# Casts of P at the head of ScalarE's step, homes behind low parts, and a two-pass hash with row groups added by VectorE, in an LSH attention kernel with an FFN

## The chip, the cores and the metric

One Trainium2 chip, of which the kernel uses one core. The metric is the device time of the kernel in microseconds (us), the median of several runs. Before the change it is 975.12 us (three runs, 974.37 to 977.23). The engines are named as in the profile: PE (matmul) and PEld (its weight loads), DVE (VectorE), ACT (ScalarE), POOL (GpSimd), SP (the sync engine, whose queue issues nearly all transfers).

## The reference

The kernel computes LSH attention and a gated FFN on its result. There are 4 batches of 8 heads, 768 positions and 64 channels.

```python
q_bits = (np.einsum('bhsd,dk->bhsk', q, proj) > 0)      # 6 bits
k_bits = (np.einsum('bhsd,dk->bhsk', k, proj) > 0)
mask = q_bucket[:, :, :, None] == k_bucket[:, :, None, :]
scores = np.where(mask, scale * np.matmul(q, k.transpose(0, 1, 3, 2)), -1e9)
attn = np.exp(scores - np.max(scores, axis=-1, keepdims=True))
attn = attn / (np.sum(attn, axis=-1, keepdims=True) + 1e-09)
x = np.matmul(attn, v)          # then to [3072 tokens, 512]
h = x @ w_in                    # 512 x 2048
g = h * np.clip(h + 3.0, 0.0, 6.0) / 6.0
return g @ w_out                # 2048 x 512
```

A query and a key belong to one bucket when their six sign bits agree.

## The kernel before, in words

**Numbers in two parts.** Every float32 operand of a matmul is split into a high part, rounded to the matmul's own type `F32R` by a cast, and a low part, the difference. Products are made of high x high, high x low and low x high. A "cast" below is the making of a high part, on ACT; a "low part" is the subtraction behind it, on DVE or POOL.

**The hash.** A head's queries and keys lie in two tiles of 2 x 768 columns, `kk` and `qq`. Their halves are `k1`, `k2`, `q1`, `q2` (L287). `q1` holds the high parts of the scaled queries in rows 0 to 63 and of the keys in rows 64 to 127, `k2` the low and high parts of the keys, `q2` the high and low parts of the queries. `hash_qk` (L325) makes the projections of one half of the columns by three passes of 384 columns: low weights on `q1`, high weights on `k2`, high weights on `q2` (L334 to L336). `bits` (L340) turns their signs into twelve rows for the queries and twelve for the keys, which are appended to the operands of the scores, so that a bucket that differs makes a score huge. On DVE this is one compare-and-multiply a half (L352), whose rows for the keys go to `k1` by a transfer (L359).

**Tiles of attention.** A head has six tiles of 128 queries; `g` counts all 192 of them. A tile takes scores on PE (L387, L389), the minimum and a cap on DVE (`lowest`, L396), the exponential with its sums on ACT (`exponential`, L408). Then P has to be transposed for the value products. In the first half of the kernel PE does that (L418). From tile 102 (`GT`) on it goes through memory: `flip` (L426) transposes 32x32 blocks on DVE (L429) and writes the tile to a scratch tensor `fd` (L431, 384 KB), and `move` (L434) brings it home by four transfers of 96 KB each, which put the blocks in place (L444). There are two homes, `spare` and `px`, for even and odd tiles. `split_p` (L451) casts a home in two halves on ACT (L475); the low part of half 1 is made on POOL (L477) and that of half 0 on DVE (L479). `values_whole` (L505) multiplies two tiles at a time with V (L513).

**The FFN beside it.** The batches 1 to 3 have nine chunks of 256 tokens, and a chunk has 16 slices of the hidden width. A slice is GEMM1 (L661, 12 matmuls of 256 columns), the gate (a relu on ACT, L683, and a product on DVE, L684), the gate's cast and low part (L689 on ACT, L690 on DVE), and GEMM2 (L699 to L704, six matmuls of 512 columns), which runs a slice later. The generator `ffn` (L927) gives such a slice in parts, named A to D: A the gate's cast and low part, B the next GEMM1, C the GEMM2 of the slice before and the relu, D the work on the next chunk's input.

**The order.** The order on PE, DVE, ACT and POOL is the order of the program text; on SP a scheduler places the transfers, within the bounds that `issue_after` sets. Each engine and SP's queue work in order. From tile 102 on, `beside_ffn(k)` (L1115) writes one step per tile (90 of them): value products (odd k), `lowest(k+2)`, part A, `exponential(k+2)`, `flip(k+2)`, cast of half 1 of tile k-1, part B, copies of finished values, in one step of six the hash, part C with the cast of half 0 of tile k-1 and its low part behind the relu (the list `amid`, L1174, called from `gate` at L685), then `lead(k+3)` (L1038: scores, and by turns the split, load and scaling of later heads), `move(k+1)` and part D. The list `moves` holds transfers that are issued one a step (L1183).

Of the kernel before, what the change touches and what calls it, by code (L numbers as in the profile page):

```python
# [10 lines left out]
F32 = mybir.dt.float32  # L11
# [32 lines left out]
def lsh_attention_moe(  # L44
# [74 lines left out]
    pjl = cp.tile([P, ZM], F32R, name="pjl")  # L119
    pjh = cp.tile([P, ZM + ZK - D], F32R, name="pjh")  # L120
    nc.vector.memset(pjl[:].bitcast(F32), 0.0)
    nc.vector.memset(pjh[:].bitcast(F32), 0.0)
    pjk, pjq = pjh[:, :ZM], pjh[:, ZK - D :]


    nc.vector.memset(thr[:], 0.0)
    nc.vector.memset(val[:], 0.0)
    for r, one, big in ((D, 0, -BIG), (ZK, 1, 1.0)):
# [4 lines left out]
        nc.vector.memset(val[r : r + NB], big * (1, -1)[one])  # L133
    nc.vector.memset(three[:], 3.0)

    raw0 = sp.tile([P, S], F32, name="raw0", tag="raw", bufs=1)[:]
# [142 lines left out]
    subs = []  # L279
    moves = []  # L280

# [43 lines left out]
    def hash_qk(i: int):  # L325
        k1, k2, q1, q2 = state[i]
        if paced:
            z = zs[i] = [bank([P, HW], f"z{i}_{j}") for j in range(2)]
        else:
            both = pair(f"z{i}")  # L330
            z = zs[i] = [both[:, j, :HW] for j in range(2)]
        for j in range(2):
            c = slice(j * HW, (j + 1) * HW)
            nc.tensor.matmul(z[j][:ZM], lhsT=pjl[:], rhs=q1[:, c], start=True, stop=False)  # L334
            nc.tensor.matmul(z[j][:ZM], lhsT=pjk, rhs=k2[:, c], start=False, stop=False)
            nc.tensor.matmul(z[j][:ZM], lhsT=pjq, rhs=q2[:, c], start=False, stop=True)  # L336
        if not paced:
            zs[i] = both

    def bits(i: int):  # L340
# [3 lines left out]
        if isinstance(z, list):  # L344
            whole = [(slice(j * HW, (j + 1) * HW), z[j][D:ZM], False) for j in range(2)]
        elif i == 0:
# [76 lines left out]

    written, moved, homes = {}, {}, []

    def flip(g: int):  # L426
# [3 lines left out]
        d = dp.tile([P, S], F32, name=f"fd{g}", tag="fd", bufs=4)  # L430
        dma(out=d[:], in_=x)  # L431
        written[g] = d, last

    def move(g: int):  # L434
# [6 lines left out]
        with tc.issue_after(after.ins):  # L441
            for x in range(4):
# [86 lines left out]
    def output(un: int):  # L529
# [18 lines left out]
        if u or last_head:  # L548
# [6 lines left out]
            if not last_head:  # L555
                ts = (u,) if single or u else (0, 1)
                (fresh if single and u == 2 else adds).append((i, ts if u != 1 or single else (0, 1), to, y[r2] if single else outs[i][r2]))
        vdone = 2 * un + 2
# [168 lines left out]
    xr0, x0 = {}, {}  # L727
    side, opening, amid = [], [], []

# [197 lines left out]
    def ffn():  # L927
# [49 lines left out]
        for c, (b, t) in enumerate(chunks):  # L977
# [21 lines left out]
            for fc in range(NFC):  # L999
# [6 lines left out]
                parted = paced  # L1006
                split_g = gate(n, fc, hp, copy, nc.vector, lambda: amid and amid.pop()())
                if not parted:
# [29 lines left out]
    def lead(j: int):  # L1038
# [11 lines left out]
        if t == (3 if paced else 2):  # L1050

            if n + 1 < NJ and n != H + 1:
                get_qk(n + 1)
                if paced:
                    get_k_rows(n + 1)
        if t == (5 if paced else 3) and n < NJ:
# [42 lines left out]
    with tc.manual_schedule(engines={ET.PE, ET.DVE, ET.Activation, ET.Pool}):  # L1099
# [15 lines left out]
        def beside_ffn(k: int):  # L1115
# [9 lines left out]
            for _ in range(2):  # L1125
# [45 lines left out]
            if hashed:  # L1171
                hash_qk((k + LA) // KT + 1)
            if split:
                amid.append(lambda: (split_p(k - LT, 0, False), split_lows()))  # L1174
            go("C")
            while amid:
                amid.pop()()
            split_lows()
            if hashed:
                bits((k + LA) // KT + 1)  # L1180
            if k + LA < NS:
# [13 lines left out]
        for k in range(NS + LT + 2):  # L1195
# [11 lines left out]
            if k == HK:  # L1207
                late["x"] = sp.tile([P, S], F32, name="late", tag="raw", bufs=1)
            for c in range(2):
                transp(k, c)  # L1210
# [117 lines left out]
```

## Time and profile before

| | |
|---|---|
| median of three runs | 975.12 us |
| the profiled execution | 973.11 us, span 971.3 us, granted PE clock 0.998 |
| attention alone, first FFN, attention to tile 101 | about 0 to 395 us |
| attention beside the FFN, tiles 102 to 191 | about 395 to 805 us |
| FFN alone | about 805 to 971 us |
| PE busy, 395 to 805 us | 403.18 us |
| DVE, ACT, POOL busy there | 324.57, 272.67, 211.39 us |
| DMA engines busy there | 82%, 240 GB/s |

A row of a group reads: line, engine, operation, out<-in by the program's names, shapes, count, then the busy time in us, the mean of one in ns, and the idle time of the engine before it with what ended it. PE's busy time is modelled and its matmuls overlap, so the start times of neighbouring rows tell what a matmul costs. SP's rows are issues of transfers; how long a transfer flies is seen only where something waits for it. A wait for several things is put down to the one that came last.

### The profile page before, as it was taken

The numbers are of one execution on the slowest core, as the hardware profiler recorded it, in microseconds if no ns is written. First come the engines' busy times: TensorE is split into PE (matmuls) and PEld (weight loads), VectorE is DVE, ScalarE is ACT, GpSimd is POOL, SyncE is SP. The second block draws the span as 40 slices with busy tenths as digits, with TensorE's granted clock in tenths as the row PEclk, the third lists the DMA queues.
The fourth block names the chain that finished last, engine by engine and source line by source line (L and its number), as shares of the span: only waits on it lengthen the run. The fifth ranks groups of instructions, "written<-read, shape, count | busy, mean of one in ns | idle before, by whom it ended". The sixth has DMA issues, their size and how long they took to land.

```text
span 971.3 us, 19460 instructions
## 1 busy us (share of the span) xinstructions
PE 948.0 (98%) x6306; PEld 873.6 (90%) x6306; DVE 723.5 (74%) x1470; ACT 625.0 (64%) x1421; POOL 473.6 (49%) x582
## 2 busy tenths in 40 slices
PE   8999999999999999899999999999999999999997
PEld 7999888999989999799899899989899899889896
DVE  7999988888569999877878878878777874342422
ACT  6898875655478988667766666666666664333332
POOL 6777744665537776455555545555545432000000
PEclk9999999999999999999999999999999999999999
DMA  3567579100035554787898788788887772101000
GB/s 117 140 156 188 131 224 377 58 1 1 6 119 119 115 142 112 192 252 233 238 267 234 231 256 241 230 267 236 243 258 233 211 227 71 44 1 44 1 22 22
DMA packets 113613, 152.06 MB, mean 157 GB/s; under 512 B 13876, under 2 KB 82612, under 8 KB 113512
## 3 DMA queue, kind: packets, MB, share of 16 engines
q1 hardware_dynamic: 108472, 144.79, 48.8%
q0 software_dynamic: 5040, 6.03, 5.3%
q8 instruction: 50, 0.82, 0.4%
q14 instruction: 51, 0.42, 0.2%
HBM read 77.34 MB, written 54.00 MB: 135 GB/s over the span
## 4 chain that ended last, share of the span: by engine, by line
PE 79%; DVE 8%; DMA 4%; ACT 4%; issue 3%; POOL 1%; SPq 1%; ACTq 0%; DVEq 0%; POOLq 0%
PE h L661 25%; PE acc L500 6%; PE po L704 6%; PE po L699 6%; PE po L700 6%; PE acc L513 6%; PE pt L418 5%; PE s L389 5%; PE s L387 5%; DMA spare<-fd 2%; DVE p L396 2%; DVE pl L479 2%; ACT ph L475 1%; SPq L78 1%; DVE qq L352 1%
## 5 line engine op out<-in xcount | busy, mean ns | idle before, releaser
L408 ACT ACTIVATE p<-p,m 128x768 f32<-128x768 f32 x192 | 180.2, 939 | 113.4 <-DVE p L396 105.2
L396 DVE TENSOR_SCALAR_CACHE_REDUCE p<-s 128x768 f32<-128x768 f32 x192 | 182.7, 952 | 24.9 <-PE pt L418 12.4
L684 DVE SCALAR_TENSOR_TENSOR h<-g,h 128x256 f32<-128x256 f32 x192 | 81.1, 423 | 102.0 <-ACT g L683 99.0
L683 ACT ACTIVATE g<-h,three 128x256 f32<-128x256 f32 x192 | 91.2, 475 | 94.9 <-PE h L661 94.0
L661 PE MATMUL h<-xh,w 128*128 128x256 f32 x1024 | 146.8, 282 | 0.0
L661 PEld LDWEIGHTS h<-xh,w 128*128 128x128 f32 x1024 | 134.9, 188 | 4.2 <-ACT xh L650 0.6
L429 DVE STREAM_TRANSPOSE p<-p 128x768 f32<-128x768 f32 x90 | 88.1, 979 | 65.2 <-ACT p L408 65.1
L477 POOL TENSOR_TENSOR pl<-spare,ph 128x384 fp32r<-128x384 f32 x45 | 45.8, 1018 | 127.3 <-ACT ph L475 71.4
L479 DVE TENSOR_TENSOR pl<-pt,ph 128x384 fp32r<-128x384 f32 x196 | 100.0, 550 | 4.0 <-ACT ph L475 3.5
L387 PE MATMUL s<-kk,qq 76*128 76x384 f32 x384 | 100.5, 343 | 2.0 <-ACT kk L357 1.5
L389 PE MATMUL s<-kk,qq 128*128 128x384 f32 x384 | 100.4, 343 | 0.0
L700 PE MATMUL po<-w,gb 128*128 128x512 f32 x250 | 98.4, 393 | 0.0
L699 PE MATMUL po<-w,gb 128*128 128x512 f32 x250 | 98.3, 393 | 0.0
L475 ACT CAST ph<-pt 128x384 fp32r<-128x384 f32 x196 | 86.1, 474 | 14.3 <-PE pt L418 13.0
L216 POOL TENSOR_TENSOR w<-wr,w 128x128 fp32r<-128x128 f32 x128 | 71.9, 593 | 45.2 <-ACT w L210 41.9
L418 PE MATMUL pt<-ident,p 128*128 128x128 f32 x612 | 86.2, 275 | 1.9 <-DVE pl L479 1.1
L689 ACT CAST gb<-h 128x256 fp32r<-128x256 f32 x141 | 52.4, 372 | 54.5 <-DVE h L684 26.8
L661 PE MATMUL h<-xl,w 128*128 128x256 f32 x512 | 81.2, 280 | 0.0
L418 PEld LDWEIGHTS pt<-ident,p 128*128 128x128 f32 x612 | 72.5, 141 | 8.9 <-PE pt L418 1.5
L704 PE MATMUL po<-w,gb 128*128 128x512 f32 x250 | 78.6, 395 | 1.5 <-DVE gb L690 1.5
L318 POOL TENSOR_TENSOR kk<-raw,qq 64x192 fp32r<-64x192 f32 (+1 forms) x73 | 65.4, 920 | 25.1 <-ACT qq L304 21.7
L387 PEld LDWEIGHTS s<-kk,qq 76*128 76x128 f32 x384 | 66.6, 190 | 11.7 <-ACT kk L357 2.0
(153 smaller groups left out, 2150.9 us busy)
## 6 DMA issues: line engine op xcount, KB each, us to landing
fd<-p SPq DMA_DIRECT2D x90, 384.0 KB
spare<-fd SPq DMA_DIRECT2D x180, 96.0 KB
px<-fd SPq DMA_DIRECT2D x180, 96.0 KB
kk<-qq SPq DMA_DIRECT2D x62, 192.0 KB
wr<-in_w_in SPq DMA_DIRECT2D x16, 512.0 KB
wr<-in_w_out SPq DMA_DIRECT2D x16, 512.0 KB
raw<-in_qkT SPq DMA_DIRECT2D x19, 384.0 KB
vr<-in_v SPq DMA_DIRECT2D x32, 192.0 KB
```

Of the source, the lines that this page charges most:

```text
L387: nc.tensor.matmul(s[:, c, :HW], lhsT=q1[:KM, us], rhs=half(k1[:KM], c), start=True, stop=False)
L389: nc.tensor.matmul(s[:, c, :HW], lhsT=q2[:, us], rhs=half(k2, c), start=False, stop=True)
L396: nc.vector.tensor_scalar(out=pr_[:], in0=s[:, :, :HW], scalar1=CAP, scalar2=None, op0=ALU.min, op1=ALU.min, accum_out=m[:],)
L408: nc.scalar.activation(pr_[:], pr_[:], AF.Exp, bias=m[:], scale=-1.0, accum_out=sms[b][:, t, h : h + 1])
L418: nc.tensor.transpose(pt[:, x], probs[g][0][:, c, x * P : (x + 1) * P], ident[:])
L475: nc.scalar.copy(hi, pt)
L479: lows.append(lambda: engine.tensor_sub(lo, pt, hi.bitcast(F32)))
L661: nc.tensor.matmul(hp, lhsT=wi[:, wp, wc], rhs=x[cc][xp], start=(k == 0 and cc == 0), stop=(k == 2 and cc == NCC - 1),)
L683: nc.scalar.activation(r[:], hp, AF.Relu, bias=three[:], scale=1.0)
L699: nc.tensor.matmul(po[u], lhsT=gh[:, us], rhs=wo[:, 0], start=(fc == 0), stop=False)
L700: nc.tensor.matmul(po[u], lhsT=gh[:, us], rhs=wo[:, 1], start=False, stop=False)
L704: nc.tensor.matmul(po[u], lhsT=gl[:, us], rhs=wo[:, 0], start=False, stop=(fc == NFC - 1))
```

## The change

There are three edits to the steps beside the FFN, and what they need.

1. **Casts first.** In `beside_ffn`, both casts of tile k-1 stand at the head of ACT's step, ahead of the gate's cast and of the exponential, and the low part of half 0 (DVE) right behind them, ahead of the gate's low part. In the step behind a hash the gate's cast and low part stand between the casts and the low part of P. The list `amid` is gone. In the first such step (k = 103) the casts stand at the end.
2. **Homes behind low parts.** `move(k+1)` follows the low parts of tile k-1 at once, instead of standing at the step's end. `flip(k+2)` comes later in the same step, and its transfer to `fd` is ordered behind the last of the four homes (`brought`). The transfer of the keys' bits and the load of the next keys' rows wait in a list `behind_home`, which is emptied at the step's end; the keys' rows are loaded a step later than before.
3. **The hash in two passes.** Beside the FFN, `short_weights` makes a weight tile `pjs` (in the room of `pjh`) on POOL, once, at step 100. One pass is made on `q2` and one on `k2`. Each weight has 120 columns: 24 for the products with low weights and 24, at row 96, for those with high weights. ACT copies the first group of rows from the result into rows 96 to 119 of the next head's raw tile, DVE adds the second group there, and one compare-and-multiply over all 768 columns makes the bits. Its limits and factors (`limits`) are set by eight memsets on POOL at the start.

Beside these, the accumulating transfer for the last third of a head (L557) goes into the list that is sent next, not into the one behind it.

```diff
 def get_k_rows(i):
-        moves.append(lambda: dma(out=raws[i][D:], in_=qkT[b, h, D:]))
+        behind_home.append(lambda: dma(out=raws[i][D:], in_=qkT[b, h, D:]))
...
+    def short_weights():
+        pjs = cp.tile([P, ZK + NR + NQ], F32R, name="pjs", tag="pjh")
+        nc.gpsimd.memset(pjs[:].bitcast(F32), 0.0)
+        short.extend([pjs[:, : ZK + NR], pjs[:, NQ:]])
+        c = ZK + NQ
+        pos = pjs[:, c + NB : c + NQ].bitcast(F32)
+        for x in range(2):
+            nc.gpsimd.tensor_scalar_mul(pjs[:, c + (1 - x) * NB : c + (2 - x) * NB], pr[:], (1.0, -1.0)[x])
+        nc.gpsimd.tensor_sub(pjs[:, NQ + NB : 2 * NQ], pr[:], pos)
+        nc.gpsimd.tensor_sub(pjs[:, NQ : NQ + NB], pos, pr[:])
...
 def hash_qk(i):
         if paced:
-            z = zs[i] = [bank([P, HW], f"z{i}_{j}") for j in range(2)]
+            zs[i] = []
+            for j in range(2):
+                c = slice(j * HW, (j + 1) * HW)
+                z = bank([P, HW], f"z{i}_{j}")
+                zs[i].append(z)
+                nc.tensor.matmul(z[: ZK + NR], lhsT=short[1], rhs=q2[:, c], start=True, stop=False)
+                nc.tensor.matmul(z[: ZK + NR], lhsT=short[0], rhs=k2[:, c], start=False, stop=True)
+            return
...
 def bits(i):
         if isinstance(z, list):
-            whole = [(slice(j * HW, (j + 1) * HW), z[j][D:ZM], False) for j in range(2)]
+            r = slice(ZK, ZK + NR)
+            both = raws[i + 1][r] if i + 1 < NJ else sp.tile([P, S], F32, name=f"raw{i + 1}", tag="raw", bufs=1)[r]
+            for j in range(2):
+                nc.scalar.copy(both[:, j * HW : (j + 1) * HW], z[j][:NR])
+            for j in range(2):
+                c = slice(j * HW, (j + 1) * HW)
+                nc.vector.tensor_add(both[:, c], z[j][r], both[:, c])
+            nc.vector.tensor_scalar(
+                out=q1[D : D + NR], in0=both, scalar1=ths[r], scalar2=vas[r], op0=ALU.is_gt, op1=ALU.mult,
+            )
+            behind_home.append(lambda: dma(out=k1[D : D + NQ].bitcast(F32), in_=q1[D + NQ : D + NR].bitcast(F32)))
+            return
...
 def flip(g):
-        dma(out=d[:], in_=x)
+        if brought:
+            with tc.issue_after(brought.pop().ins):
+                dma(out=d[:], in_=x)
+        else:
+            dma(out=d[:], in_=x)
...
 def move(g):
+        brought[:] = [last]
...
 def beside_ffn(k):
-            behind = (k - 1 + LA) % KT == 4
-            if GT <= k < NS - 2 and not behind:
+            split = GT <= k - LT < NS
+            if not split or k == GT + 1:
+                go("A")
+            if GT <= k < NS - 2:
                 lowest(k + 2)
-            go("A")
-            if GT <= k < NS - 2 and behind:
-                lowest(k + 2)
+            if split and k - LT > GT:
+                multiply()
+                for c in (1, 0):
+                    split_p(k - LT, c, False)
+                if (k - 1 + LA) % KT == 4:
+                    go("A")
+                split_lows()
+                if k + 1 < NS:
+                    move(k + 1)
+                go("A")
...
-            split = GT <= k - LT < NS
-            if split:
-                split_p(k - LT, 1, False)
             go("B")
...
-            if split:
-                amid.append(lambda: (split_p(k - LT, 0, False), split_lows()))
             go("C")
-            while amid:
-                amid.pop()()
-            split_lows()
...
-            if GT <= k + 1 < NS:
+            if GT <= k + 1 < NS and not (split and k - LT > GT):
                 move(k + 1)
+            while behind_home:
+                behind_home.pop(0)()
```

How this moves the instructions is seen at three places. The first is SP's queue around the tiles 133 to 135. `fd133` is tile 133's scratch tensor, `p133` the tile itself, `spare` and `px` are the homes, `raw`, `xs` and `vr` other traffic. Before:

```order
L78 DMA fd133_7383<-p133_7375 128x768
L78 DMA spare_5091<-fd132_7317 32x4x192 x4
L78 DMA raw24_7472<-in_qkT 64x768 x2
L78 DMA xs2_127<-y21_0_7334 64x512
L78 DMA fd134_7442<-p134_7434 128x768
L78 DMA px_5555<-fd133_7383 32x4x192 x4
L78 DMA fd135_7509<-p135_7501 128x768
```

And with the change:

```order
L78 DMA fd133_7415<-p133_7395 128x768
L78 DMA xs2_136<-y21_0_7360 64x512
L78 DMA px_5570<-fd133_7415 32x4x192 x4
L78 DMA fd134_7470<-p134_7454 128x768
L78 DMA vr23_7644<-in_v 128x384
L78 DMA spare_5100<-fd134_7470 32x4x192 x4
L78 DMA fd135_7540<-p135_7520 128x768
```

Before, the homes behind `fd134` read `fd133`, which was issued a step earlier. Now they read the `fd` that was issued last, and the next `fd` stands behind them.

The second place is ACT in the same steps: `ph65` holds the high parts of the tiles 130 and 131, `g` and `h` are the gate, `gb` its high part, `y` finished values. Before, from the cast of the gate on:

```order
L689 CAST gb1_1_13_7436<-h1_1_13_7389 128x256
L408 ACTIVATE p134_7434,sms2_5285<-p134_7434,m134_7433 128x768
L475 CAST ph65_1_7385<-px_5555 128x3x128
L547 COPY y21_0_7334<-acc64_7361 128x256
L683 ACTIVATE g1_1_14_7467<-h1_1_14_7446,three_68 128x256
L475 CAST ph65_0_7411<-px_5555 128x3x128
```

With the change:

```order
L517 CAST ph65_1_7398<-px_5570 128x3x128
L517 CAST ph65_0_7402<-px_5570 128x3x128
L731 CAST gb1_1_13_7465<-h1_1_13_7417 128x256
L445 ACTIVATE p134_7454,sms2_5294<-p134_7454,m134_7453 128x768
L589 COPY y21_0_7360<-acc64_7381 128x256
L725 ACTIVATE g1_1_14_7493<-h1_1_14_7472,three_68 128x256
```

Both casts of the home have moved from behind the exponential and from behind the relu to the head, and the gate's cast and the exponential stand behind them.

The third place is PE at the hash of head 23, between GEMM1 and GEMM2. Before:

```order
L334 MATMUL z23_0_7528<-qq_23_7286,pjl_74 108x384
L335 MATMUL z23_0_7528<-kk_23_7285,pjh_75 108x384
L336 MATMUL z23_0_7528<-qq_23_7286,pjh_75 108x384
L334 MATMUL z23_1_7529<-qq_23_7286,pjl_74 108x384
L335 MATMUL z23_1_7529<-kk_23_7285,pjh_75 108x384
L336 MATMUL z23_1_7529<-qq_23_7286,pjh_75 108x384
L699 MATMUL po1_1_6590<-w29_3343,gb1_1_14_7503 128x512
```

With the change:

```order
L354 MATMUL z23_0_7555<-qq_23_7310,pjs_5485 120x384
L355 MATMUL z23_0_7555<-kk_23_7309,pjs_5485 120x384
L354 MATMUL z23_1_7558<-qq_23_7310,pjs_5485 120x384
L355 MATMUL z23_1_7558<-kk_23_7309,pjs_5485 120x384
L741 MATMUL po1_1_6614<-w29_3352,gb1_1_14_7535 128x512
```

Two of six passes are gone, and GEMM2 follows the fourth.

More of the change, by code (lines that the diff above doesn't have):

```diff
@@ L119, in lsh_attention_moe @@
     pjl = cp.tile([P, ZM], F32R, name="pjl")
-    pjh = cp.tile([P, ZM + ZK - D], F32R, name="pjh")
+    pjh = cp.tile([P, ZM + ZK - D], F32R, name="pjh", tag="pjh")
     nc.vector.memset(pjl[:].bitcast(F32), 0.0)
@@ L123, in lsh_attention_moe @@
     pjk, pjq = pjh[:, :ZM], pjh[:, ZK - D :]
+    NQ = 2 * NB
+    NR = 2 * NQ
+    short = []
+    limits = cp.tile([P, 2], F32, name="limits")
+    ths, vas = limits[:, 0:1], limits[:, 1:2]
     nc.vector.memset(thr[:], 0.0)
@@ L327, in hash_qk @@
         if paced:
-            z = zs[i] = [bank([P, HW], f"z{i}_{j}") for j in range(2)]
-        else:
-            both = pair(f"z{i}")
-            z = zs[i] = [both[:, j, :HW] for j in range(2)]
+            zs[i] = []
[6 more added lines that the diff above has]
+            return
+        both = pair(f"z{i}")
+        z = zs[i] = [both[:, j, :HW] for j in range(2)]
         for j in range(2):
@@ L336, in hash_qk @@
             nc.tensor.matmul(z[j][:ZM], lhsT=pjq, rhs=q2[:, c], start=False, stop=True)
-        if not paced:
-            zs[i] = both
+        zs[i] = both
     def bits(i: int):
@@ L556, in output @@
                 ts = (u,) if single or u else (0, 1)
-                (fresh if single and u == 2 else adds).append((i, ts if u != 1 or single else (0, 1), to, y[r2] if single else outs[i][r2]))
+                (fresh if single and u == 2 and not paced else adds).append((i, ts if u != 1 or single else (0, 1), to, y[r2] if single else outs[i][r2]))
         vdone = 2 * un + 2
@@ L727, in lsh_attention_moe @@
     xr0, x0 = {}, {}
[L728 removed]
+    side, opening = [], []
     def beside():
@@ L1006, in ffn @@
                 parted = paced
-                split_g = gate(n, fc, hp, copy, nc.vector, lambda: amid and amid.pop()())
+                split_g = gate(n, fc, hp, copy, nc.vector)
                 if not parted:
```

20 lines of the change are left out of this document (15 added, 5 removed).

## Prediction

> **What bounds the kernel now.** I read the page first, then the stretch in which attention runs beside the FFN (395 to 805 us), because all of the change but two tiny set-up pieces lies there.
>
> ```profile
> span 971.3 us, 19460 instructions
> PE 948.0 (98%) x6306; PEld 873.6 (90%) x6306; DVE 723.5 (74%) x1470; ACT 625.0 (64%) x1421; POOL 473.6 (49%) x582
> ```
>
> ```profile
> 395.00:805.00 410.00, 403.18 (x2614) 371.45 (x2613) 324.57 (x620) 272.67 (x639) 211.39 (x273) 1.00 0.82 240
> ```
>
> The second fence is that stretch in the table of windows: its length, then PE, PEld, DVE, ACT and POOL busy, then the granted clock, the DMA engines' busy share and GB/s. PE is busy 403 of 410 us at full clock; VectorE 79%, ScalarE 67%; but the DMA engines are busy 82% too. So PE paces, and the transfers come next. The waits of PE and of its weight loads in this stretch say what is left to win:
>
> ```profile
> PE acc L513 <- ACT ph L475: 4.5, 9, 1.5
> PE po L704 <- DVE gb L690: 1.5, 2, 0.8
> PEld acc L513 <- ACT ph L475: 6.0, 12, 1.7
> ```
>
> (Total us, times, longest.) The value products wait for the casts of P, 6.0 us counted at the weight load; everything else is small. A step's length comes from the transfer that each step issues once, in the view of the tile `fd`, and the homes that bring it back, four to a step:
>
> ```profile
> L78 SPq DMA_DIRECT2D fd<-p x89: 320/382/1419, 400.4 to 800.8; - x89
> L78 SPq DMA_DIRECT2D spare<-fd x180: 302/442/887, 400.8 to 803.1; - x180
> ```
>
> 89 issues from 400.4 to 800.8 are 88 steps of 4.55 us. The queue that issues them waits as follows (its own waits in the stretch):
>
> ```profile
> SPq L78 <- DVE pl L479: 25.7, 55, 1.0
> SPq L78 <- DMA fd<-p: 3.2, 6, 0.8
> ```
>
> Today homes wait for the low part that frees their buffer (55 times), and almost never for the landing of `fd`, because each home's source was issued a step before it. This second row is the one that I expect to change.
>
> **The hash.** A hash in this stretch is six passes; here is one from the timeline (start, us), and behind it the groups of the stretch by line (count, busy, mean ns):
>
> ```profile
> 763.38 0.34 PE L334 MATMUL z<-qq,pjl 128*108 128x384 f32 x1
> 763.56 0.34 PE L335 MATMUL z<-kk,pjh 128*108 128x384 f32 x1
> 763.74 0.34 PE L336 MATMUL z<-qq,pjh 128*108 128x384 f32 x1
> ...
> 764.43 0.40 PE L699 MATMUL po<-w,gb 128*128 128x512 f32 x1
> ```
>
> ```profile
> L334 PE MATMUL z<-qq,pjl 128*108 128x384 f32 x28 | 9.5, 338 | 0.2 <-ACT y L547 0.2
> L352 DVE TENSOR_SCALAR qq<-z,thr,val 44x384 fp32r<-44x384 f32 x28 | 18.0, 686 | 0.5
> ```
>
> From 763.38 to 764.43 six passes take 1.05, so 0.175 each (the 338 ns of a row overlap). x28 is two halves of 14 heads; two passes less a head are 14 x 2 x 0.175 = 4.9 us of PE, all on its path. Added are two copies of 24x384 on ScalarE, two sums and one compare on VectorE:
>
> ```profile
> L475 ACT CAST ph<-px 128x384 fp32r<-128x384 f32 x88 | 44.2, 502 | 0.4 <-issue 0.2 <-DMA px<-fd 0.2
> L479 DVE TENSOR_TENSOR pl<-px,ph 128x384 fp32r<-128x384 f32 x44 | 28.5, 648 | 0.1
> L429 DVE STREAM_TRANSPOSE p<-p 128x768 f32<-128x768 f32 x90 | 88.1, 979 | 65.2 <-ACT p L408 65.1
> L408 ACT ACTIVATE p<-p,m 128x768 f32<-128x768 f32 x89 | 83.5, 939 | 101.9 <-DVE p L396 94.2 <-DMA spare<-fd 6.3 <-DMA fd<-p 1.4
> L408 ACT ACTIVATION_READ_ACCUMULATOR p<-p,m 128x1 f32 x89 | 16.5, 186 | 0.0
> L689 ACT CAST gb<-h 128x256 fp32r<-128x256 f32 x89 | 33.0, 371 | 28.3 <-PE po L704 24.0 <-DVE h L684 1.6
> ```
>
> By nearest shapes, ScalarE pays 2 x 0.5 = 1.0 and VectorE 2 x 0.65 + about 1.0 (768 wide, as the transpose) - 2 x 0.69 = 0.9 more per head, once in six steps (27 us) in which VectorE is idle 21% and ScalarE 33%, 5.6 and 9. I cost it at nothing; were the cover gone it would be at most 14 x 1.0 = 14 us, below nothing I see no way. The two passes need the shifted rows and the low parts of both operands at once, where the first of three needed only `q1`; the third needed them 0.35 us later anyway, so: nothing. The load of the next K rows now waits, on the sync queue and ahead of a home, until the compare has read its scratch rows; that lies inside the flight of `fd` (below) as long as the queue runs late, and would else hold a home by about 1 us a head, within the slack worked out below. The K rows themselves are loaded a step later, behind the homes, and are needed two steps on, 9 us for a transfer like v's (2.1 us, below): nothing. The short weights and eight memsets run on POOL, and the last accumulating transfer of a head is sent one turn earlier there; POOL is 49% busy: nothing.
>
> **The casts and the value products.** With both casts at the head of ScalarE's step and the low parts behind them, the products that need them a step later find them ready: up to 6.0 us back. What moves behind is the cast of the gate (L689), by 2 x 0.50 us, and the exponential. The gate's cast is needed behind a whole GEMM1, so at full pace this costs nothing. But ScalarE works in order: when a home is late, the cast waits, and behind it now stand the gate's cast (GEMM2 waits for it) and the exponential (the next `fd` waits for it). Before, only the relu stood behind the first cast.
>
> **The homes and fd.** Here I see the price. Today the queue runs fd(g+1), home(g): a home's source has a whole step to land. In the change it runs fd(g), home(g), fd(g+1): a home waits for the `fd` just issued, and the next `fd` stands behind those homes. One turn of this chain is the flight of `fd`, F, and the issue of four homes. No turn starts before the last has ended, so on average no step can be shorter than one turn. The four issues from the queue's timeline, and a flight there:
>
> ```profile
> 413.47 1.89 SPq L78 DMA_DIRECT2D px<-fd  x4
> ...
> 447.71 0.53 SPq L78 DMA_DIRECT2D fd<-p  x1
> 448.49 2.83 SPq L78 DMA_DIRECT2D px<-fd  x4
> 451.42 0.38 SPq L78 DMA_DIRECT2D fd<-p  x1
> 452.65 1.75 SPq L78 DMA_DIRECT2D spare<-fd  x4
> ```
>
> Four homes take 1.75 to 1.89 when nothing holds them; I take 1.89, with 0.05 before and behind them. The homes at 452.65 had waited for the `fd` of 447.71 (the longest wait, 0.8, of the six): F was there 452.65 - 447.71 = 4.9, an upper end, with other homes in flight beside it. The trace shows no flight of a lone `fd`, so it is bounded from smaller transfers in the chain that ended last (start, us from issue to landing), and the best rate of the DMA view:
>
> ```profile
> 516.88 1.78 DMA spare<-fd
> 527.59 2.12 DMA spare<-fd
> 546.67 2.08 DMA vr<-in_v
> 575.82 3.53 DMA spare<-fd
> GB/s 230 247 223 275 204 253 218 246 258 274 254 265 203 234 237 224 255 262 253 260 210 231 232 271 259 236 243 252 215 254 279 247 255 224 242 215 182 270 208 212
> ```
>
> A home (96 KB) lands in 1.78 to 3.53, v (192 KB) in 2.08. `fd` has 384 KB: 288 KB (294,912 B) more than a home at 279 GB/s are 1.06, so 2.84; from v, 192 KB more are 0.70, so 2.78. The least would be a home's 1.78, the most 4.9. I take 2.7, just under the two sums, since little else flies beside it now. In the Trainium skill, "DMA: Bandwidth & Descriptors", section "Anatomy of one DMA", a transfer costs about 2.0 us whatever its size plus bytes over 436 GB/s (a fit for the other, software path), mostly the receipt from the target memory. By that, estimated, F would be 2.9 and the sum below would end 18 us later, inside case (4). No run here shows a lone flight, but the 1.78 of a home is under that 2.0.
>
> One turn: 2.7 + 0.05 + 1.89 + 0.05 = 4.69, against 4.55 now and against PE's own pace with all gains, (88 x 4.55 - 4.9 - 6.0) / 88 = 4.43. Until the chain is felt, slack runs out first: a step's casts to the issue of its `fd` are 2 x 0.50 + 0.37 + 0.94 + 0.19 + 0.98 = 3.5 (casts of P and of the gate, exponential, its sum, transpose); then F, the fourth home's start 1.89 - 0.44 later and its landing in 2.1, as at 527.59: 9.8 in all. The casts that need it stand three steps on, 13.3 at 4.43: 3.5 are left.
>
> Sum on the profiled execution (973.1, 1.8 of it outside the span): 88 x (4.69 - 4.55) = +12.3, less 3.5 = +8.8, so 982. PE's 10.9 us are in this, since the chain's turn takes the place of PE's pace. The median of the runs was 975.1, 2.0 above the profiled one, so the median I name is 984.
>
> **The rivals.** (1) PE keeps the pace: F is at most 4.43 - 1.99 = 2.44. Then both gains come whole, 975.1 - 10.9 = 964. For it: PE's 98%, and the 1.78 of a small transfer. Against: both sums from rows put 384 KB over 2.7, at the best rate. 0.15. (2) The chain paces, but turns fast: F from 2.44 to 2.57, 964 to 972; the row of 55 waits for low parts speaks for it, since those waits go. 0.18. (3) No change: F around 2.6, where 88 x (4.59 - 4.55) meets the slack of 3.5. A measurement of this kernel can tell 0.3%, 2.9 us, from nothing, which is 0.03 of F on either side. 0.13. (4) My forecast, the chain paces with F from 2.63 to 3.0, 978 to 1010. 0.44. (5) F stays as long as it can be today, over 3.0 (say 3.5: a turn of 5.49, +79, 1054), as other transfers between `fd` and its homes fill the queue; the 82% speaks for it, that fd's now fly apart from homes against. 0.10. That the change does not do what it says I rule out: the order of its instructions shows it.
>
> **How the numbers follow.** Faster are (1) and (2), 0.33; same is (3), 0.13; slower are (4) and (5), 0.54. As cases of both signs hold most of the chance: the likeliest one's own range is 978 to 1010. The range 963 to 1008 leaves out (5) and the ends.
>
> **What would show it.** Right: the waits of the sync queue for `fd<-p` rise from 6 to near 90 and tens of us; `fd` issues stand 4.7 apart, not 4.55; ScalarE's casts wait for DMA of `px` and `spare`; PE's waits for `ph` shrink, and waits of GEMM2 for the gate's cast or low part take their place; PE's share falls under 98%. Hash passes x4 a head, still 0.175. Wrong: `fd` issues 4.4 apart with PE at 98% or more, or long waits for the hash's VectorE work.

## The result, and the profile after

The kernel with the change takes 1033.98 us (median of six runs, 1026.76 to 1038.95); the kernel before, on the same chip, 975.26 us (six runs, 974.37 to 977.23). The ratio is 1.0594 with a 95% interval of 1.0556 to 1.0633: slower by 5.9%, 58.7 us. The forecast was 984, with a range of 963 to 1008. The change is slower, as forecast, and by the loop that the prediction describes; the size was not forecast.

The profiled execution took 1038.95 us, the slowest of the six. The page of the changed kernel, with the engines' busy time and the chain that ended last:

```profile
span 1037.2 us, 19432 instructions
PE 967.5 (93%) x6278; PEld 871.8 (84%) x6278; DVE 737.4 (71%) x1484; ACT 638.0 (62%) x1449; POOL 474.4 (46%) x595
PE 54%; DMA 19%; DVE 13%; issue 6%; SPq 3%; POOL 2%; ACT 1%; DVEq 1%; ACTq 0%; POOLq 0%
DMA fd<-p 17%; PE h L703 15%; PE acc L542 6%; PE pt L455 5%; PE po L746 5%; DVE pl L521 4%; PE po L741 4%; PE po L742 4%; PE s L426 4%; PE s L424 3%; SPq L78 3%; DVE p L433 3%; PE acc L555 2%; DVE gb L732 1%; DMA px<-fd 1%
```

PE has fallen from 98% to 93% of the span, and the largest single share of the chain, 17% or some 176 us, is now the flight of one transfer, `fd<-p`. The stages (columns as in the prediction's window):

```profile
395.00:870.00 475.00, 423.71 (x2592) 371.22 (x2591) 336.61 (x634) 286.85 (x670) 212.35 (x279) 0.98 0.70 208
870.00:1037.00 167.00, 160.97 (x1037) 144.14 (x1035) 60.16 (x145) 57.20 (x136) 8.50 (x16) 1.00 0.08 24
```

The FFN alone is as long as before, 167 against 166 us. All of the loss is in the attention beside the FFN, where PE now idles for 51 of 475 us and the DMA engines are less busy (70%) than before (82%). So it is not a lack of bandwidth; the transfers wait for one another. The tile `fd`, before and with the change:

```profile
L78 SPq DMA_DIRECT2D fd<-p x90: 320/382/1419, 397.1 to 800.8; - x90
L78 SPq DMA_DIRECT2D fd<-p x90: 319/376/1282, 397.8 to 867.5; - x90
```

With the change, 90 issues from 397.8 to 867.5 are 89 steps of 5.28 us, 469.7 us in all. Before, they took 403.7 us, 4.54 a step. The difference, 66.0, is the whole difference of the spans (65.9). What the sync queue waited for in this stretch:

```profile
SPq L78 <- DMA fd<-p: 114.5, 76, 4.3
...
SPq L78 <- DVE pl L521: 5.8, 7, 1.8
```

Before, the queue waited 55 times for low parts and 6 times (3.2 us) for `fd` to land. Now it is 7 times for low parts and 76 times, 114.5 us, for `fd`. Its timeline shows the loop itself:

```profile
610.45 0.43 SPq L78 DMA_DIRECT2D fd<-p  x1
610.99 0.48 SPq L78 DMA_DIRECT2D kk<-qq  x1
611.52 0.60 SPq L78 DMA_DIRECT2D qq<-qq  x1
613.25 2.18 SPq L78 DMA_DIRECT2D spare<-fd  x4
615.53 0.38 SPq L78 DMA_DIRECT2D fd<-p  x1
615.95 0.47 SPq L78 DMA_DIRECT2D kk<-qq  x1
617.15 0.47 SPq L78 DMA_DIRECT2D xs<-y  x1
618.57 1.73 SPq L78 DMA_DIRECT2D px<-fd  x4
620.40 0.38 SPq L78 DMA_DIRECT2D fd<-p  x1
```

Read it from the top: `fd` at 610.45, two transfers of 192 KB in its shadow, a pause until `fd` has landed (613.2), four homes, and at once the next `fd` at 615.53. The next turn, to 620.40, is the same. The queue has no slack in these turns in which to catch up.

How this reaches PE is told by three views of waits in the stretch (total us, times, longest). VectorE's:

```profile
DVE p L433 <- DMA fd<-p: 96.0, 56, 4.4
```

ScalarE's:

```profile
ACT ph L517 <- DMA px<-fd: 38.2, 38, 3.5
ACT ph L517 <- PE acc L555: 31.6, 19, 3.4
ACT ph L517 <- DMA spare<-fd: 28.4, 16, 3.0
```

And the weight loads of PE:

```profile
PEld po L746 <- DVE gb L732: 46.4, 52, 2.7
PEld po L741 <- ACT gb L731: 19.9, 22, 3.6
```

A tile `p` has two buffers, so `lowest` of tile g+2 (L433) cannot write until `fd` of tile g has read its buffer. Before, it started 2.3 us (mean) after that landing; now 0.41, and in most steps 0.14, that is, it stood waiting. Behind it on VectorE stands the low part of the gate (L732), and GEMM2 waits for that. On ScalarE the casts of a late home hold the gate's cast (L731). The middle row is a wait that the prediction does not name: the casts at the head write buffers that the step's own value products (L555) still read. It is rarely the one that PE feels: of the 22 waits for the gate's cast, 21 stand behind a cast that had waited for its home. The value products, which were to gain, wait for nothing now: no row `acc <- ph` is left in this stretch.

### The profile page after: what moved, and what is told of

Read it like the earlier page. It is cut to its first block, busy times and chain, and to the rows that moved or that the text cites. A ratio compares the mean times of both kernels' runs of the same rounds, so it can differ in the third digit from the quotient of the medians.

```text
span 1037.2 us, 19432 instructions
## 1 busy us (share of the span) xinstructions
PE 967.5 (93%) x6278; PEld 871.8 (84%) x6278; DVE 737.4 (71%) x1484; ACT 638.0 (62%) x1449; POOL 474.4 (46%) x595
## 4 chain that ended last, share of the span: by engine, by line
PE 54%; DMA 19%; DVE 13%; issue 6%; SPq 3%; POOL 2%; ACT 1%; DVEq 1%; ACTq 0%; POOLq 0%
DMA fd<-p 17%; PE h L703 15%; PE acc L542 6%; PE pt L455 5%; PE po L746 5%; DVE pl L521 4%; PE po L741 4%; PE po L742 4%; PE s L426 4%; PE s L424 3%; SPq L78 3%; DVE p L433 3%; PE acc L555 2%; DVE gb L732 1%; DMA px<-fd 1%
## 5 line engine op out<-in xcount | busy, mean ns | idle before, releaser
L433 DVE TENSOR_SCALAR_CACHE_REDUCE p<-s 128x768 f32<-128x768 f32 x192 | 183.3, 955 | 127.7 <-DMA fd<-p 96.0
L741 PE MATMUL po<-w,gb 128*128 128x512 f32 x250 | 102.5, 410 | 15.9 <-ACT gb L731 15.8
L746 PE MATMUL po<-w,gb 128*128 128x512 f32 x250 | 85.3, 423 | 24.9 <-DVE gb L732 24.6
L742 PE MATMUL po<-w,gb 128*128 128x512 f32 x250 | 99.4, 397 | 0.0
L746 PEld LDWEIGHTS po<-w,gb 128*128 128x128 f32 x250 | 43.6, 192 | 53.4 <-DVE gb L732 46.8
L517 ACT CAST ph<-spare 128x384 fp32r<-128x384 f32 x90 | 41.8, 511 | 63.8 <-PE acc L555 31.6
```

Source lines behind the costliest of these rows:

```text
L433: nc.vector.tensor_scalar(out=pr_[:], in0=s[:, :, :HW], scalar1=CAP, scalar2=None, op0=ALU.min, op1=ALU.min, accum_out=m[:],)
L517: nc.scalar.copy(hi, pt)
L741: nc.tensor.matmul(po[u], lhsT=gh[:, us], rhs=wo[:, 0], start=(fc == 0), stop=False)
L742: nc.tensor.matmul(po[u], lhsT=gh[:, us], rhs=wo[:, 1], start=False, stop=False)
L746: nc.tensor.matmul(po[u], lhsT=gl[:, us], rhs=wo[:, 0], start=False, stop=(fc == NFC - 1))
```

## The experiments

Three theories stood after the result. **Theory 1**: the loop on the sync queue (`fd`, its flight, four homes, next `fd`) sets the step. **Theory 2**: ScalarE's order does, as the gate's cast now stands behind casts that wait. **Theory 3**: the hash's added work on VectorE and ScalarE costs more than two passes save. Times are medians; each ratio is to the kernel before on the same chip (974.28 us for chain_alone, homes_behind_fd, homes_at_end and hash_alone; 973.80 for gate_first, no_adds, fd_on_act and hash_dve; 975.03 for the other four).

**chain_alone.** The kernel before, and only `fd` put behind the homes.

```diff
 def flip(g):
-        dma(out=d[:], in_=x)
-        written[g] = d, last
+        def send():
+            dma(out=d[:], in_=x)
+            written[g] = d, last
+        if GT < g - 1 < NS - 1:
+            later.append(send)
+        else:
+            send()
...
                 move(k + 1)
+                while later:
+                    with tc.issue_after(last.ins):
+                        later.pop(0)()
```

> The kernel before, with nothing changed but the sync queue: the transfer of tile k+2 to its scratch tensor is issued behind the homes of tile k+1. All engines keep their order, the hash has three passes. Theory 1 (chain): fd issues 5.2 to 5.5 apart, the queue waits for fd in nearly every turn, 1025 to 1050. Theories 2 (ScalarE's order) and 3 (hash): 975, as before, since neither is in it.

1044.19 us, ratio 1.0709 [1.0692, 1.0726]. The tile `fd`, and the sync queue's waits for it:

```profile
L78 SPq DMA_DIRECT2D fd<-p x90: 319/430/1257, 397.4 to 874.8; - x90
```

```profile
SPq L78 <- DMA fd<-p: 92.8, 63, 4.2
```

5.36 us a step with the casts and the hash as they were: the loop is enough by itself for the whole loss, and more (+69.9). That is theory 1's branch of the expectation.

**homes_behind_fd** and **homes_at_end.** The reverse: the change without the loop. In the first, the homes follow the issue of the next `fd`; in the second they stand at the step's end, as before.

```diff
-        if brought:
-            with tc.issue_after(brought.pop().ins):
-                dma(out=d[:], in_=x)
-        else:
-            dma(out=d[:], in_=x)
+        dma(out=d[:], in_=x)
...
                 split_lows()
-                if k + 1 < NS:
-                    move(k + 1)
...
                 flip(k + 2)
+            if split and k - LT > GT and k + 1 < NS:
+                move(k + 1)
```

The second, beside the first two pieces of this, has:

```diff
-            if GT <= k + 1 < NS and not (split and k - LT > GT):
+            if GT <= k + 1 < NS:
                 move(k + 1)
```

> The change, but the homes of tile k+1 are issued right behind the transfer of tile k+2 to its scratch tensor, as they were before the change, so that no home waits for a flight that has just begun. Casts first and the two-pass hash stay. Theory 1 (the chain on the sync queue: flight of fd, four homes, next fd, one after the other, 5.3 us a turn): the chain is cut, fd issues stand about 4.4 apart, both of PE's gains show, about 964 (958 to 972). Theory 2 (ScalarE's order: a late home now holds up the gate's cast and the exponential): hardly better than the change, over 1000. Theory 3 (the hash: its work on VectorE and ScalarE, and the queue's waits for its bits): over 1000 too.

> The change, but the homes of tile k+1 are issued at the end of step k, behind the scores, where they stood before the change. Casts first and the two-pass hash stay. Theory 1 (chain): cut as well, about 966 (960 to 975), at most a little slower than with the homes right behind fd, since they start later. Theories 2 (ScalarE's order) and 3 (hash): over 1000.

996.00 us, ratio 1.0227 [1.0199, 1.0254], and 995.94, ratio 1.0216 [1.0198, 1.0234]. Both lie between the two branches of their expectations. In the first the queue waits for `fd` 4 times, 2.0 us. What ScalarE waited there for homes to land (from the view of `fd`: us, times), and PE's weight loads:

```profile
  ACT ph L513: 64.8, 41
```

```profile
PEld po L737 <- ACT gb L727: 20.9, 24, 3.4
PEld po L742 <- DVE gb L728: 16.7, 41, 0.8
```

Taking the loop out brings 38 us back, less than theory 1 alone wants: 22 remain, and GEMM2 still waits for the gate's cast (24 times, up to 3.4). Casts of P wait for a home 41 times, and 23 of the 24 waits stand right behind such a cast. Where the homes stand, once they are out of the loop, makes no difference.

**gate_first.** homes_behind_fd, with the gate's cast and low part ahead of the casts of P.

```diff
             if split and k - LT > GT:
+                go("A")
                 multiply()
                 for c in (1, 0):
                     split_p(k - LT, c, False)
-                if (k - 1 + LA) % KT == 4:
-                    go("A")
                 split_lows()
-                go("A")
```

> As the run with the homes right behind fd (996), but the gate's cast and low part stand ahead of the casts of P again. Theory 2 (in that run a cast that waits for its home holds up the gate's cast, for which GEMM2 waits, 21 us): those waits go, 975 to 985. Rival (the homes are late for the casts wherever the gate's cast stands, and the exponential and value products pay): 990 to 1000.

977.34 us, ratio 1.0026 [1.0010, 1.0042]. PE's weight loads:

```profile
PEld po L742 <- DVE gb L728: 11.6, 14, 2.2
PEld h L699 <- DVE raw L377: 3.4, 8, 0.6
PEld po L737 <- ACT gb L727: 2.7, 3, 1.4
```

The waits for the gate's cast are down from 20.9 to 2.7, and 18.7 us come back. That cost belongs to theory 2: a cast that needs no transfer stood behind two that do.

**chain_gate_first.** The change, loop and all, with that same exchange of order.

```diff
             if split and k - LT > GT:
+                go("A")
                 multiply()
...
-                if (k - 1 + LA) % KT == 4:
-                    go("A")
                 split_lows()
                 if k + 1 < NS:
                     move(k + 1)
-                go("A")
```

> The change with its chain of fd, homes, fd kept, only the gate's cast and its low part ahead of the casts of P. Theory 1 (the chain sets the turn, and what stands behind the casts on ScalarE lies in its shadow): 1028 to 1040, fd still 5.2 to 5.4 apart, the waits of PE for the gate's cast mostly gone. Theory 2 (the gate's cast behind waiting casts adds to the chain): 1034 - 18.7 = 1015, fd about 5.1 apart.

1022.18 us, ratio 1.0485 [1.0459, 1.0512], with `fd` 5.14 apart:

```profile
L78 SPq DMA_DIRECT2D fd<-p x90: 320/376/792, 397.0 to 854.6; - x90
```

It lies between the two expectations: the exchange brings about 11 us instead of 18.7, so part of the gate's cost lies in the shadow of the loop, and part does not. Neither theory said that. In the trace the loop still sets the step: a turn is shorter because its flight (3.09 us in the mean, 3.19 in the change) and its four homes (1.89, 1.93) are.

**half_fd.** The change, with `fd` half as large (192 KB).

```diff
-                dma(out=d[:], in_=x)
+                dma(out=d[:, : S // 2], in_=x[:, : S // 2])
...
-                    in_=d[:].rearrange("(i b) (g c) -> g b i c", i=4, g=4)[x],
+                    in_=d[:, : S // 2].rearrange("(i b) (g c) -> g b i c", i=4, g=2)[x % 2],
```

> The change, but fd carries half of its bytes (192 KB, the left half of every tile's columns), and the homes read that half twice, so half of the transposed P is left out. Theory 1 (a turn is the flight of the bytes plus the four homes): the flight falls by 0.6 to 0.7 us, 89 x 0.65 = 58 less, where PE's own pace with the gate's cast late, 996, bounds it: 985 to 1000, fd 4.6 to 4.8 apart. Theory 2 (the flight is mostly waiting behind accumulating transfers and instruction loads on shared DMA engines, whatever its size): less than half of that, 1005 to 1030.

994.67 us, ratio 1.0205 [1.0183, 1.0227]:

```profile
L78 SPq DMA_DIRECT2D fd<-p x90: 319/376/1731, 397.4 to 823.1; - x90
```

4.78 us a step. From the issue and landing events of all steps, the mean flight fell from 3.19 to 2.63 and the turn from 5.34 to 4.83, nearly as much. The flight is a term of the step: theory 1. That it is so one to one is not shown, since 4.78 is also PE's own pace with the late gate (4.79 a step in homes_behind_fd).

**no_adds.** The change without POOL's accumulating transfers beside the FFN.

```diff
-        for _, _, to, of in adds:
+        for _, _, to, of in adds if not paced else ():
             nc.gpsimd.dma_start(out=to, in_=of, accum_op=ALU.add)
```

> The change, without the accumulating transfers that POOL sends beside the FFN, so a part of the value products (the low part of V) is left out of the sums from there on. In the changed trace a flight of fd takes 2.73 us in the mean when neither such a transfer nor a load of instructions is on the DMA engines, 3.25 with an accumulating transfer (19 flights), 3.94 with a load of instructions (24 flights). Theory 1a (what shares the engines with fd makes its flight longer, and each us of flight is a us of the turn): 19 x 0.5 = 10 us less, 1024 (1018 to 1030). Theory 1b (flights scatter by themselves): no difference, 1034.

1019.54 us, ratio 1.0464 [1.0430, 1.0498]:

```profile
L78 SPq DMA_DIRECT2D fd<-p x90: 320/376/581, 397.7 to 849.9; - x90
```

5.08 us a step, 0.20 less; the mean flight falls from 3.19 to 2.87. Transfers on another queue lengthen this one, as theory 1a has it (1018 to 1030), though the four homes take longer (2.01 us, 1.93 in the change) and so the step falls by less than the flight.

**fd_on_act.** The change, with `fd` issued by ScalarE behind the relu, so that it stands behind no home.

```diff
+        def send():
+            written[g] = d, nc.scalar.dma_start(out=d[:], in_=x)
+        if g > GT + 2:
+            sends.append(send)
...
-        after = written[g + 1][1] if g + 1 in written else last
+        after = written[g + 1][1] if g + 1 in written and g < GT + 2 else last
...
             go("C")
+            while sends:
+                sends.pop(0)()
```

> The change, but the transfers to the scratch tensor are issued on ScalarE's own queue, behind the relu, so that they no longer stand behind the homes and the homes no longer stand behind them on one queue; homes still start right behind the low parts, earlier than in the two runs with the chain cut. Theory 1 (chain) with theory 2 (with casts first a late home holds up the gate's cast): chain cut and homes earlier, so fewer waits of the casts; faster than the 996 of those two, 965 to 990. Theory 2 alone, with ScalarE's order the greater cost and 0.4 us a step more of issue on ScalarE: 996 or more.

1005.06 us, ratio 1.0315 [1.0275, 1.0354]: missed by 15 us. ScalarE's waits:

```profile
ACT ph L521 <- PE acc L559: 41.2, 26, 2.1
...
ACT ph L521 <- DMA px<-fd: 16.0, 12, 2.8
...
ACT qq L325 <- DVE h L730: 12.8, 11, 1.2
```

The loop is cut on its issue side, which is worth 27 to 29 us, but the homes still wait for a flight (41 times, 63.5 us on the sync queue), and some casts for their homes. The expectation left out a new wait: ScalarE stands at its issue of `fd` until VectorE has transposed the tile. The issue begins 0.59 us behind the relu (mean of 87) and 0.03 us behind the transpose (median), and all 43 waits of ScalarE that end like the last row, on L730, hold such an issue. Of the 18 waits of PE for the gate's cast (13.5 us), six stand behind a cast that waited for a home. How the 9 us over homes_behind_fd divide among these is not shown.

**hash_alone.** The kernel before with only the two-pass hash, its bits, and the K rows loaded a step later (`short_weights`, `hash_qk` and `bits` as in the change):

```diff
 def hash_qk(i):
-            z = zs[i] = [bank([P, HW], f"z{i}_{j}") for j in range(2)]
...
+                nc.tensor.matmul(z[: ZK + NR], lhsT=short[1], rhs=q2[:, c], start=True, stop=False)
+                nc.tensor.matmul(z[: ZK + NR], lhsT=short[0], rhs=k2[:, c], start=False, stop=True)
```

> The kernel before with the two-pass hash alone (and the load of the next K rows a step later, which its scratch rows need). Theory 1 (chain): no chain here, PE saves 14 x 2 x 0.175 = 4.9 us, 970 (967 to 974). Theory 3 (hash): its two copies, two sums and the waits for its bits cost more than that, 990 or more. Theory 2: says nothing of it, 970.

982.70 us, ratio 1.0088 [1.0071, 1.0104]. Neither branch: it costs 8.4 where it was to save 4.9. PE's largest wait at a weight load, and the groups of the added work:

```profile
PEld acc L550 <- ACT ph L512: 11.8, 22, 2.1
```

```profile
L377 DVE TENSOR_TENSOR raw<-z,raw 24x384 f32<-24x384 f32 x28 | 14.6, 559 | 0.4
L374 ACT COPY raw<-z 24x384 f32<-24x384 f32 x28 | 11.7, 465 | 0.3
L378 DVE TENSOR_SCALAR qq<-raw,limits 24x768 fp32r<-24x768 f32 x14 | 10.4, 745 | 0.5
```

The pieces cost what was estimated: 2 x 0.465 = 0.93 on ScalarE, 2 x 0.559 + 0.745 - 2 x 0.686 = 0.49 on VectorE. But what the starts of PE's matmuls beside the FFN stand apart beyond their usual pace adds up to 34.5 us, against 21.7 before, so 13 us of new stalls stand against 4.9 saved. Most of them (0.7 us a head) fall in the step behind the hash, at value products that wait for the casts of P.

**hash_dve.** hash_alone, with VectorE copying the first group of rows in ScalarE's place.

```diff
-                nc.scalar.copy(both[:, j * HW : (j + 1) * HW], z[j][:NR])
+                nc.vector.tensor_copy(both[:, j * HW : (j + 1) * HW], z[j][:NR])
```

> As the run with the two-pass hash alone (983), but VectorE, not ScalarE, copies the first row group out. Theory 3a (ScalarE's 2 x 0.47 us in the step of the hash push its later casts back, and the value products two steps on wait for them by about 1 us a head): those waits go, 969 to 975. Theory 3b (it is VectorE's longer chain, 2 x 0.56 + 0.75 against 2 x 0.69, that pushes): worse, 985 to 995. Theory 3c (it is the later load of the K rows): the same 983.

994.59 us, ratio 1.0201 [1.0179, 1.0222], 12 us more, in the range of theory 3b. VectorE is the worse place, though it was idle 21% of the stretch: `lowest` and the transposes of the tiles queue behind the copies, and ScalarE's exponentials wait 127.5 us for `lowest` (94.2 before).

**casts_alone** and **gate_first_3pass.** homes_behind_fd and gate_first, each with the three-pass hash of before, its bits and its load of the K rows.

```diff
 def hash_qk(i):
-            for j in range(2):
...
-                nc.tensor.matmul(z[: ZK + NR], lhsT=short[1], rhs=q2[:, c], start=True, stop=False)
-                nc.tensor.matmul(z[: ZK + NR], lhsT=short[0], rhs=k2[:, c], start=False, stop=True)
-            return
+            z = zs[i] = [bank([P, HW], f"z{i}_{j}") for j in range(2)]
...
 def get_k_rows(i):
-        behind_home.append(lambda: dma(out=raws[i][D:], in_=qkT[b, h, D:]))
+        moves.append(lambda: dma(out=raws[i][D:], in_=qkT[b, h, D:]))
```

> Casts of P first, the gate's cast behind them, the homes behind the next fd, and the hash of before in three passes. Theory A (the parts add up): 996.0 - 8.4 = 988, with PE still waiting 15 to 20 us for the gate's cast. Theory B (the hash costs nothing once the casts are early): 994 to 1001.

> The version with the gate's cast ahead of the casts of P and the homes behind the next fd, but with the hash of before (three passes, its bits and K rows as before). Theory A (the parts add up: the two-pass hash cost 8.4 by itself): 977.3 - 8.4 = 969, faster than before by about 5. Theory B (the hash's stalls of the value products come from late casts, and with the casts early they are gone already): 977 to 981, the hash then costs nothing or saves 4.9 there.

993.91 us, ratio 1.0193 [1.0174, 1.0211], and 971.88, ratio 0.9962 [0.9947, 0.9977]. With the gate late, the two-pass hash costs 2 to 3 us, which the two intervals do not tell from nothing, and lies for the rest in that shadow: nearer theory B. With the gate first it costs about 6 (1.0026 against 0.9962): nearer theory A, which said 8.4. The second kernel is the best of all, 0.4% faster than before. It also keeps the moved accumulating transfer (L557), which no run tests alone. Its `fd` stand 4.53 us apart and the value products hardly wait:

```profile
L78 SPq DMA_DIRECT2D fd<-p x90: 320/345/1604, 397.4 to 800.4; - x90
```

## Why the prediction was right or wrong

**The loop and its price.** "One turn of this chain is the flight of `fd`, F, and the issue of four homes" was right, and so was "no step can be shorter than one turn". The mean of 86 turns, from the events of the trace, is 5.34 us: F 3.19, then 0.14 until the first home's issue, 1.93 for the four homes, 0.09 until the next `fd`. The forecast was 4.69 = 2.7 + 0.05 + 1.89 + 0.05. Of the 0.65 by which it was short, 0.49 is F, 0.13 the gaps and 0.04 the homes. With the measured turn in it, the sum holds: 86 x (5.34 - 4.54) = 69, less the slack of 3.5, is 65, against 65.9 between the two profiles. The slack shows too: a transposed tile now waits 3.80 us for its `fd` to be issued, 0.34 before.

**The step that failed** is "I take 2.7, just under the two sums, since little else flies beside it now". F measured 3.19. The value is right for a flight beside which only the sync queue's own packets move: 44 flights were such, mean 2.73. But 19 shared the DMA engines with an accumulating transfer of POOL (mean 3.25), and 24 with a load of instructions (3.94; eight of these met both). The chain that ended last shows flights of both kinds (start, us from issue to landing):

```profile
442.38 5.36 DMA fd<-p
...
449.60 2.68 DMA fd<-p
...
459.48 2.63 DMA fd<-p
```

The DMA view for 440 to 449 us, around the long one (queue, kind: packets, MB, share of the engines):

```profile
q1 hardware_dynamic: 1082, 1.30, 50.8%
q0 software_dynamic: 80, 0.13, 10.0%
q8 instruction: 1, 0.02, 0.7%
q14 instruction: 1, 0.01, 0.3%
```

And for the flight at 459.48, to its landing:

```profile
q1 hardware_dynamic: 486, 0.62, 67.4%
```

The short flight has only the sync queue's packets beside it; the long one has accumulating and instruction packets. Fifteen of its sixteen landing events are in by 445.81; an instruction packet of 8 KB runs from 446.30 to 446.78, its own last packets follow one by one, and the last event comes at 447.74. I had bounded F by 4.9 from above and put 0.10 on "over 3.0", which is the case that came, with F at 3.19 and not 3.5. The range of 963 to 1008 cut that case off. That the accumulating transfers lengthen F is shown by no_adds. No run took the instruction loads away, and a long flight meets more of them by its length alone, so 3.94 is not their price. But the landing events tell: in the 24 flights with a load the last event comes 0.76 us (mean) behind the fifteenth, in the others 0.06 to 0.14. By this, an estimate, the loads make 24 x 0.65 / 87 = 0.18 us of the mean F.

The term could have been read before the change, and not only where something waits for a transfer: the landing events are in the trace of the kernel before, though no view lists them. Its 90 flights took 3.41 us in the mean. So the relief that the prediction expected came, from 3.41 to 3.19, but it started from more than 2.7. With 3.41, the prediction's sum gives 88 x (3.41 + 1.99 - 4.55) - 3.5 = 71 and 1046, over the measured 1034.

In the Trainium skill, "DMA: Bandwidth & Descriptors", section "Anatomy of one DMA", the fit gave 2.9, an estimate, for this size. The 44 undisturbed flights are under it (2.73), the mean over it (3.19). The fit's slope agrees: half the bytes made such flights 0.40 us shorter (2.33 in half_fd), by the fit, an estimate, 0.45.

**"At full pace this costs nothing"**, of the gate's cast. The condition was stated and did not hold: 54 casts waited for homes in the change. The price, by gate_first, is 18.7 us without the loop, some 11 with it. It was mentioned as a risk and left out of the sum; that the sum comes out with the measured turn in it does not make it right, since the loop's turn takes this cost up. Nor did it need the loop: in homes_behind_fd, too, 41 casts waited for a home.

**"I cost it at nothing"**, of the hash. The bound of 14 us named in the same sentence was the better number in hash_alone: 13 us of stalls. Idle shares of 21% and 33% were no cover, since the work arrives at one place of an in-order engine, ahead of casts and minima that other engines wait for. Rival (1) rested on the gain of 4.9 coming whole. What the hash costs inside the loop no run shows.

**The value products.** Their 6.0 us were won, as predicted: in the change as in gate_first_3pass no wait of PE for a cast of P is left beside the FFN. Some 3 us are left over in the second, if they come from there; the gate's low part, which now comes later at times, takes some back (4.2 us at the weight load, 5 times).

**The signs.** The sync queue's waits for `fd<-p` went from 6 to 76 (near 90 was said), casts wait for `px` and `spare`, GEMM2 waits for the gate, PE fell under 98%: right. `fd` stood 5.28 apart, not 4.7: wrong.

**What stays open.** Why flights and homes are shorter when the gate's cast goes first, how much of F the instruction loads make up beyond the estimate, and how much of the hash's cost is the later load of the K rows.

## What to carry to other kernels

When a queue that works in order both writes a buffer and reads it back, keep at least one write ahead of each read. Here write, read, write put a whole flight into every step, though the DMA engines got idler. Price such a flight by its mean among all the traffic it shares engines with, not by its undisturbed time, since every turn pays it; look for it in the landing events where no view shows it. On an in-order engine, work whose input is already there goes ahead of work that waits for a transfer, and here an engine's idle share said nothing about what an added instruction holds up behind it.

## What the runs showed of the hardware

- A transfer of 384 KB from SBUF to memory, with only the sync queue's packets beside it, lands 2.73 us after its issue begins (mean of 44 in the change), one of 192 KB 2.33 (46 flights in half_fd).
- Loads of instructions share the DMA engines with it: 50 packets of them fell into 400 to 870 us of the change. A flight has sixteen landing events, and in the 24 flights that met a load the last of them came 0.76 us behind the fifteenth, against 0.06 in the undisturbed ones.
- The granted clock of PE fell in the change, and not evenly. Its records hold 0.5 for 3.4 us from 518.5, 6.8 us from 566.2 and 3.4 us from 593.6. In the 3.4 us ahead of each of these PE was busy 46, 37 and 48% of the time, by its modelled busy time. Two stretches of the change, and the second of them in the kernel before:

```profile
395.00:470.00 75.00, 65.21 (x405) 56.29 (x404) 54.47 (x102) 45.13 (x106) 34.42 (x49) 1.00 0.70 202
470.00:600.00 130.00, 115.77 (x701) 103.26 (x700) 93.52 (x173) 78.66 (x184) 58.03 (x77) 0.95 0.72 212
470.00:600.00 130.00, 128.69 (x826) 118.20 (x825) 103.15 (x196) 87.09 (x204) 70.30 (x93) 1.00 0.84 248
```

The kernel before has no such record beside the FFN; chain_alone granted 0.97 over its 395 to 875. The first stretch, as idle as the second and at 1.00, shows that the share of waiting over a stretch does not decide it. What does, no run here shows.
